# A fused gated-attention and gated-FFN kernel: a new order of all its steps, new buffers, and 309 instead of 534 dummy matmuls

## The chip, the cores and the metric

The kernel runs on one core of one Trainium2 chip. The metric is device time in microseconds (us) of one execution; lower is better. Before the change it is 286.42 us, the median of three runs (286.03 to 288.17).

Engine names in the profile: PE is TensorE (matmuls), PEld its weight loads, DVE VectorE, ACT ScalarE, POOL GpSimd, SP SyncE, which here only issues transfers. L948 means line 948 of the kernel file.

## The reference, cut to what matters

```python
def _attn_ref(q, k, v, a_re, a_im):               # 4 batches, 8 heads, 768 steps, head size 48
    mag = np.sqrt(a_re * a_re + a_im * a_im)
    scale = np.minimum(mag, 0.999) / (mag + 1e-06)
    a_re_n, a_im_n = (a_re * scale, a_im * scale)
    ...
    for t in range(S):                            # a complex decay of a 48x48 state
        ar, ai = a_re_n[:, :, t, :, None], a_im_n[:, :, t, :, None]
        new_re = ar * S_re - ai * S_im
        new_im = ar * S_im + ai * S_re
        S_re, S_im = (new_re + k[t] v[t]^T, new_im)   # shortened
        y[:, :, t] = q[t] . S_re                      # shortened

def _moe_ref(x, w_gate, w_val, w_out):            # x 3072x384, w_gate and w_val 384x1536, w_out 1536x384
    gate = 1.0 / (1.0 + np.exp(-(x @ w_gate)))
    return (gate * (x @ w_val)) @ w_out           # shortened
```

x is y with its heads put side by side. Everything is f32 at the borders.

## The kernel before

The sequence is cut into chunks of 128 steps, so there are 24 slabs (6 chunks of 4 batches). The slabs go through the FFN in groups of 1, 1, 2, 4, 4, 4, 4, 2 and 2. Each slab first goes through its attention part: loads of a_re and a_im (steps `lr`, `la`), squares and logarithms and angles on ScalarE, cumulative sums as matmuls with a triangular matrix (`cl`, `ct`), products of q and k with a magnitude (`qke`, on GpSimd, for slab 0 on VectorE) and with cosine and sine (`ks`, `qs`, on VectorE), then transposes (`tp`; from slab 13 on they are transfers) and score, state and output matmuls (`sc`, `kv`, `y`). A group then does twelve gate and twelve value blocks (`pg`, `pv`), the tanh of each gate block (ScalarE), the product (`p`, VectorE) and the output matmuls (`po`).

All of it is a list of steps, and a table gives each step one sort key. The keys are no times on the chip: the program sorts by them, and each engine gets its instructions, and SP and GpSimd their transfers, in that order.

```python
SIZES = [1, 1, 2, 4, 4, 4, 4, 2, 2]
TIMES = {"consts": [...], "wg": [28.263, 7.549, 23.318], ..., "la": [0.86, 2.2, 20.947, ...], ...}
SLOTS = {"qk": "043210341243030213403124", ...}   # which buffer each tile of a kind takes, in order
WARM = {('cl', 0): 90, ('ct', 0): 44, ..., ('pg', 7, 9): 2}   # 534 in all
...
        order = sorted(self.steps, key=lambda k: (at[k], self.rank[k]))
```

The loads, the square, and the two kinds of product that share SBUF:

```python
    def dma_in(dst, src, b, c):                          # 192 KB, issued by SP
        nc.sync.dma_start(
            heads(dst), src[b, :, c * L:(c + 1) * L].rearrange("h t d -> t h d"))
    ...
                nc.scalar.activation(out=T[SQ], in_=T[A][:, :, s],      # sq: needs lr and la
                                     func=FT.Square)
    ...
                eng(g).tensor_tensor(out=T[QK], in0=T[QK], in1=T[EE],   # qke, on GpSimd
                                     op=ALU.mult)
    ...
                    nc.vector.tensor_tensor(                            # ks and qs, on VectorE
                        out=T[SL][i].rearrange(...)[:, :, :, 0:D],
                        in0=heads(T[QK][:, i]).unsqueeze(2).broadcast_to([L, H, 2, D]),
                        in1=T[CS].rearrange("p r (h d) -> p h r d", d=D),
                        op=ALU.mult)
```

The carry of a slab to the next chunk (`hop`) is a transfer issued by GpSimd that adds into its destination ("carry transfer"). The weights come as nine blocks (`wg`, `wv`, `wo`, three each), also issued by GpSimd. The end of the program walks the order and puts dummy matmuls, zero times zero into the tile that the step is about to overwrite, ahead of some steps:

```python
        for key in order:
            ...
            for _ in range(WARM.get(key, 0)):
                nc.tensor.matmul(warm_of(tiles[st[2][0]]), zero, zero, start=True,
                                 stop=True)
            st[0](tiles)
```

They are meant to keep TensorE's clock from falling while it would wait anyway; what taking them out does is measured under b_nodum.

## Time and profile before

| | before |
|---|---|
| time, median of 3 runs | 286.42 us |
| span of the profiled run | 282.5 us |
| TensorE busy | 260.3 us in 2586 matmuls, 534 of them dummies |
| VectorE, ScalarE, GpSimd busy | 197.2, 200.3, 158.4 us |

TensorE is the bound, so what counts is the time in which it does no real work: it stands, it works at half clock, or it does dummies. The page's slices, the stretches and the largest wait are shown in the prediction below. TensorE's further waits in the kernel before (columns: who waited, for whom; us in total, times, longest us):

```profile
PE tp L824 <- DVE kst L786: 3.4, 2, 2.4
PE tp L825 <- DVE qst L786: 1.3, 2, 0.6
PE ct L741 <- ACT ee L661: 1.1, 1, 1.1
```

And the stretch from 40 to 80 us (columns: borders and length, busy us and instructions of PE, weight loads, DVE, ACT and POOL, granted clock, DMA share, GB/s):

```profile
40.00:80.00 40.00, 35.20 (x458) 29.43 (x455) 19.81 (x48) 26.29 (x53) 21.87 (x22) 0.91 0.90 160
```

PE looks well used here, but 35.20 us of busy time hold dummies and work at half clock.

### The profile page before, as it was taken

How to read it: one execution, taken by the hardware profiler on the slowest of the kernel's cores; microseconds unless marked ns; L12 is line 12 of the kernel's file. 1: busy time of each engine (PE TensorE's matmuls, PEld its weight loads, DVE VectorE, ACT ScalarE, POOL GpSimd, SP SyncE). 2: the span in 40 equal slices, each digit the busy share in tenths (PEclk: the TensorE clock that was granted, in tenths of full speed). 3: DMA queues.
4: the chain of work that ended last, by engine and by line, in shares of the span. 5: the costliest groups of instructions: out<-in, count | busy, mean ns of one | idle time of the engine just before them, and what ended most of it. 6: DMA issues, size and time to landing. Idle time of an engine off the chain costs nothing.

```text
span 282.5 us, 6759 instructions
## 1 busy us (share of the span) xinstructions
PE 260.3 (92%) x2586; PEld 179.7 (64%) x2586; DVE 197.2 (70%) x364; ACT 200.3 (71%) x340; POOL 158.4 (56%) x170
## 2 busy tenths in 40 slices
PE   8956994999998999999999999799999999998995
PEld 8735783888767766545774456454457545577784
DVE  3155553672478989898795897798788686697553
ACT  3993992478998997789953999674899559924240
POOL 0604981445968889947999717945449704803000
PEclk9999997799999999999999999999999999999999
DMA  7999999889489944596347769858997744074001
GB/s 146 200 180 194 167 200 195 170 177 207 60 116 201 208 97 57 100 212 139 83 91 121 157 134 210 143 90 129 222 218 105 127 102 102 9 150 107 30 30 56
DMA packets 175344, 38.46 MB, mean 136 GB/s; under 512 B 167992, under 2 KB 175312, under 8 KB 175312
## 3 DMA queue, kind: packets, MB, share of 16 engines
q1 hardware_dynamic: 170688, 34.46, 64.2%
q0 software_dynamic: 4624, 3.57, 8.6%
q8 instruction: 20, 0.33, 0.5%
q14 instruction: 12, 0.10, 0.1%
HBM read 31.01 MB, written 4.76 MB: 127 GB/s over the span
## 4 chain that ended last, share of the span: by engine, by line
PE 35%; ACT 22%; DMA 13%; POOL 9%; SPq 8%; issue 7%; DVE 4%; ACTq 0%; POOLq 0%; DVEq 0%
PE o L984 8%; PE g L948 8%; DMA a<-in_a_im_dram 8%; PE v L948 8%; SPq L579 6%; ACT L1012 5%; ACT sq L605 3%; PE ct L741 2%; PE cl L652 2%; ACT g L958 2%; ACT lm L632 2%; POOL lm L611 2%; DMA qkT<-qst 2%; POOL qk L714 2%; ACT cr L764 2%
## 5 line engine op out<-in xcount | busy, mean ns | idle before, releaser
L958 ACT ACTIVATE g<-g 128x512 f16<-128x512 f32 (+2 forms) x108 | 47.2, 455 | 48.8 <-PE g L948 40.8
L964 DVE SCALAR_TENSOR_TENSOR p<-g,v 128x512 f16<-128x512 f16 (+2 forms) x108 | 52.4, 506 | 32.0 <-PE v L948 15.3
L948 PE MATMUL v<-xt,wv 128*128 128x512 f16 (+2 forms) x324 | 60.9, 313 | 4.6 <-ACT g L958 4.2
L948 PE MATMUL g<-xt,wg 128*128 128x512 f16 (+2 forms) x324 | 59.9, 311 | 1.0 <-ACT g L958 0.5
L984 PE MATMUL o<-wo,p 128*128 128x384 f16 (+1 forms) x300 | 55.5, 319 | 0.0
L714 POOL TENSOR_TENSOR qk<-qk,ee 128x768 f32<-128x768 f32 x23 | 44.7, 1976 | 18.7 <-DMA qk<-in_q_dram 10.9
L611 POOL TENSOR_TENSOR lm<-sq 128x384 f32<-128x384 f32 x23 | 25.4, 1119 | 36.5 <-ACT sq L605 36.3
L948 PEld LDWEIGHTS <-wv 128*128 128x128 f16 x324 | 29.9, 100 | 22.5 <-issue 5.4
L948 PEld LDWEIGHTS <-wg 128*128 128x128 f16 x324 | 30.2, 99 | 21.6 <-issue 4.0
L1012 ACT ACT_TABLE_LOAD x31 | 39.8, 1283 | 0.5
L1018 PEld LDWEIGHTS <-zero 128*128 128x128 f16 x534 | 34.1, 102 | 5.6 <-issue 3.5
L851 DVE TENSOR_TENSOR mst<-sc,c_t 128x512 f16<-128x512 f32 x48 | 32.1, 684 | 6.6 <-PE sc L843 6.4
L984 PEld LDWEIGHTS <-p 128*128 128x128 f16 x300 | 27.0, 97 | 14.1 <-issue 0.9
L643 POOL TENSOR_TENSOR a<-a 128x768 f32<-128x768 f32 (+1 forms) x12 | 20.8, 1746 | 20.3 <-ACT a L637 15.4
L605 ACT ACTIVATE sq<-a 128x768 f32<-128x768 f32 x24 | 20.1, 841 | 14.0 <-DMA a<-in_a_im_dram 13.3
L786 DVE TENSOR_TENSOR kst<-qk,cs 128x768 f16<-128x768 f32 x24 | 23.5, 978 | 9.2 <-ACT cs L778 3.8
L786 DVE TENSOR_TENSOR qst<-qk,cs 128x768 f16<-128x768 f32 x24 | 23.4, 980 | 0.0
L741 PE MATMUL ct<-a,c_t 128*128 128x384 f32 x48 | 20.5, 512 | 1.8 <-ACT ee L661 1.1
L652 PE MATMUL cl<-lm,c_t 128*128 128x384 f32 x48 | 20.4, 514 | 0.8 <-DMA c_t<-glk_c 0.4
L831 DVE COPY qkT<-tp 128x1024 f16<-128x1024 f16 x26 | 17.5, 685 | 3.1 <-PE tp L825 3.0
L733 POOL DMA_DIRECT2D a<-cr x20 | 17.6, 1006 | 2.6 <-ACT a L721 2.2
L747 DVE TENSOR_SCALAR r<-ct 128x384 f16<-128x384 f32 x24 | 12.9, 551 | 8.1 <-PE ct L741 8.0
(64 smaller groups left out, 429.3 us busy)
## 6 DMA issues: line engine op xcount, KB each, us to landing
a<-in_a_re_dram SPq DMA_DIRECT2D x24, 192.0 KB
a<-in_a_im_dram SPq DMA_DIRECT2D x24, 192.0 KB
qk<-in_k_dram SPq DMA_DIRECT2D x24, 192.0 KB
v<-in_v_dram SPq DMA_DIRECT2D x24, 192.0 KB
qk<-in_q_dram SPq DMA_DIRECT2D x24, 192.0 KB
out_dram<-ot SPq DMA_DIRECT2D x23, 192.0 KB
wg<-in_moe_w_gate_dram POOLq DMA_DIRECT2D x3, 384.0 KB, 6.1
wv<-in_moe_w_val_dram POOLq DMA_DIRECT2D x3, 384.0 KB, 7.8
```

The lines of the kernel that those rows point to most:

```text
L605: nc.scalar.activation(out=T[SQ], in_=T[A][:, :, s], func=FT.Square)
L611: eng(g).tensor_tensor(out=T[LM][:, s], in0=T[SQ][:, 0], in1=T[SQ][:, 1], op=ALU.add)
L714: eng(g).tensor_tensor(out=T[QK], in0=T[QK], in1=T[EE], op=ALU.mult)
L741: nc.tensor.matmul(T[CT][:, :HD], wt_t, T[A][:, 1, s], start=True, stop=False, skip_group_check=True)
L786: nc.vector.tensor_tensor(out=T[SL][i].rearrange("p h (r x) -> p h r x", r=2)[:, :, :, 0:D], in0=heads(T[QK][:, i]).unsqueeze(2) .broadcas ...
L851: nc.vector.tensor_tensor(out=T[MS], in0=T[SC], in1=msk_t.unsqueeze(1).broadcast_to([L, 4, L]), op=ALU.mult)
L948: nc.tensor.matmul(T[ACC][:, :nt], w[:, j, fb * 128:fb * 128 + 128], T[XT][:, j, :nt], start=(j == 0), stop=(j == 2))
L958: nc.scalar.activation(out=T[G16][:, :nt], in_=T[PG][:, :nt], func=FT.Tanh, scale=0.5)
L964: nc.vector.scalar_tensor_tensor(out=T[PT][:, fb, :nt], in0=T[G16][:, :nt], scalar=1.0, op0=ALU.add, in1=T[PV][:, :nt], op1=ALU.mult)
L984: nc.tensor.matmul(T[PO][:, :wd], T[PT][:, fb, s * L:(s + 1) * L], wo16[:, fb, c0:c0 + wd], start=(fb == 0), stop=(fb == NFB - 1))
L1012: nc.scalar.preload_act_table_set(SETS[key[1]])
L1018: nc.tensor.matmul(warm_of(tiles[st[2][0]]), zero, zero, start=True, stop=True)
```

## The change

The intent is a new order of all steps in which VectorE's products do not stand beside runs of GpSimd instructions behind a carry transfer. Two slabs are through their attention part when the first gate block starts, and fewer dummies are needed. Only the three tables change: the keys of every kind of step, the buffers, the dummies. The diff, cut to a few of its some 330 lines:

```diff
 TIMES = {
     "wg": [
-        28.263, 7.549, 23.318],
+        34.405, 6.316, 29.967],
     "wo": [
-        37.677, 33.061, 38.497],
+        37.806, 46.233, 43.463],
     "la": [
-        0.86, 2.2, 20.947, 18.967, 22.867, 32.518, 40.682, 17.017, 57.834,
+        2.2, 0.45, 14.098, 15.058, 19.858, 17.938, 27.738, 25.755, 50.107,
     "lk": [
-        3.16, 8.421, 6.04, 23.827, 16.057, 52.074, 50.154, 48.796, 84.272,
+        7.461, 3.16, 5.08, 18.898, 56.053, 40.133, 40.543, 57.013, 62.417,
     ... (every other kind of step as well)
 SLOTS = {
-    "qk": "043210341243030213403124",
+    "qk": "043210342130420411041302",
     ...
 WARM = {
-    ('cl', 0): 90,
-    ('ct', 0): 44,
+    ('cl', 0): 11,
+    ('ct', 0): 45,
     ...
+    ('pg', 0, 11): 34,
     ... (534 to 309 in all)
```

The table grows by three lines, so a line number of the code behind it is 3 higher after: L786 becomes L789, L948 L951, L1018 L1021.

## The prediction

> **What bounds the kernel now.** I read the page's busy line and slices first, then TensorE's costs by form, its waits, the chain, and at last the order of the steps in both programs.
>
> The page says that TensorE is the bound, and the slices say where it is not at work. Columns: engine, then the busy tenths of 40 slices of 7.06 us.
> ```profile
> span 282.5 us, 6759 instructions
> PE 260.3 (92%) x2586; PEld 179.7 (64%) x2586; DVE 197.2 (70%) x364; ACT 200.3 (71%) x340; POOL 158.4 (56%) x170
> PE   8956994999998999999999999799999999998995
> PEclk9999997799999999999999999999999999999999
> DMA  7999999889489944596347769858997744074001
> ```
> Losses are in the first 57 us: there TensorE has holes, its clock falls once (slices 7 and 8), and DMA is full. From 57 us on TensorE is nearly full, and only less work on it, or fewer holes, can help.
>
> The stretches, with the borders put where I need them: 37.09 us is where the first gate block (line 948) starts. Columns after the borders: length, then busy us (instructions) of PE, weight loads, DVE, ACT, POOL, then granted clock, DMA share, GB/s.
> ```profile
> 0.00:37.09 37.09, 28.79 (x370) 24.26 (x371) 14.72 (x33) 26.82 (x40) 17.08 (x24) 1.00 1.02 180
> 37.09:60.00 22.91, 18.50 (x257) 16.64 (x256) 13.37 (x32) 11.52 (x31) 9.78 (x10) 0.85 1.09 186
> 100.00:250.00 150.00, 146.79 (x1248) 85.91 (x1246) 122.87 (x204) 117.68 (x187) 100.31 (x106) 1.00 0.67 126
> ```
> The largest single hole, from TensorE's waits and from the chain between 30 and 50 us:
> ```profile
> PE v L948 <- ACT g L958: 4.2, 1, 4.2
> ...
> 32.65 14.51 DMA a<-in_a_im_dram
> ...
> 47.23 0.84 ACT sq L605
> 48.07 0.17 ACT g L958
> 48.24 0.04 issue
> 48.29 0.80 PE v L948 x6
> ```
> A load of a_im for slab 5, issued at 32.65 us, landed 14.5 us later. ScalarE is in order: its square of that slab stood ahead of a tanh of group 0, so the tanh came at 48.07 us, and TensorE stood still for 4.2 us. The clock then fell to half from 46.25 to 53.08 us (the trace's clock records).
>
> The products on VectorE (line 786) and on GpSimd (line 714), min/median/max in ns:
> ```profile
> L786 DVE TENSOR_TENSOR kst<-qk,cs x24: 948/958/1444, 18.7 to 248.6; 128x768 f16<-128x768 f32 x24
> L714 POOL TENSOR_TENSOR qk<-qk,ee x23: 1805/1819/2618, 22.4 to 244.1; 128x768 f32<-128x768 f32 x23
> ```
> The longest kst product started at 111.86 us within a qk product of GpSimd, was followed on GpSimd by a carry transfer (line 733) that ended at 113.23, and itself ended at 113.31.
>
> **What the Trainium skill says.** Three places.
> "SBUF — State Buffer", section "Who interferes with whom": a VectorE instruction with two SBUF inputs contends with a GpSimd instruction that reads SBUF, and the later one waits. The trace agrees: 4 of the 48 kst and qst products are long (1026, 1196, 1404 and 1444 ns against 950 to 960), each beside GpSimd work.
> "TensorE: Matmul & The Clock Gate", Part 1: the clock halves after an idle window of about 3.4 us and comes back after a busy one; 128-column matmuls then start 107 against 56 ns apart. The trace agrees: dummies start 107 ns apart until 5.3 us, then 56; the half-rate record lasts 6.83 us after the 4.2 us hole.
> "DMA: Bandwidth & Descriptors", "Issuing engines are not separate DMA queues": what SP and GpSimd issue runs on the same DMA engines and interleaves. Here that is the cause of the 14.5 us: five weight blocks from GpSimd were issued from 30.3 to 40.0 us.
>
> **The change part by part.** No operation of the computation changes: all 2052 real matmul passes stay, and so do the 364 VectorE instructions. What changes is the order of every engine's queue, the buffers, the dummies (534 to 309) and ScalarE's table loads (31 to 28). I use the keys of the step table for order alone.
>
> *Cost of TensorE's work.* From the groups by form, at back-to-back pace: a gate or value block of three matmuls is 0.647 us at 512 columns, 0.328 at 256, 0.167 at 128; four output matmuls 0.650; cl and ct 0.70 each; the smaller ones 0.16 to 0.45. Summed over all steps that is 218.9 us. Dividing it at the first gate block by the order of steps gives 9.0 + 209.9 us before the change, 10.3 + 208.6 us after it, since slab 1 is now through its attention part when the gates start.
>
> *Dummies.* They fill 33.0 us, 0.062 us each. Placed before/after the first gate: 289/245 now, 118/191 in the new order. Those before the first gate fill time in which TensorE waits anyway and cost nothing; the 54 fewer after it save 54 x 0.062 = 3.3 us, as they stand for waits that the new order is meant not to have.
>
> *The kernel before as a sum.* 37.1 to the first gate + 209.9 real + 245 x 0.062 = 15.2 dummies + 6.5 slow matmuls (busy 231.5 after the first gate, less the two; 2.4 of them are the 4.8 us worked at half clock) + 4.2 the hole + 6.3 other holes + 3.3 from the last matmul to the end = 282.5.
>
> *First gate.* Before, it waits for its activations; its weights had landed at 15.3 us. After, the first gate block is number 11, so it needs the third block of w_gate. In the order of issue 26 loads of 192 KB and 4 weight blocks come up to and with it. The page's queue rows (64.2% of the span for 34.46 MB, 8.6% for about nine weight blocks) make 1.03 us per load and 2.7 per block: 2.0 + 26 x 1.03 + 4 x 2.7 = 39.6. The same sum for the first block of w_gate before (23 loads, 4 blocks) gives 36.5, and it landed at 36.0. So 39.1, and the gate starts at about 39.3: **2.2 us later**, an estimate.
>
> *The hole.* The last load of slab 5 is SP's 23rd transfer instead of its 33rd and comes ahead of all but two weight blocks; it will not stop a tanh. That takes 4.2 us of hole and 2.4 us of half clock. But the later weight blocks are now tight: w_gate's first block should land at 41.5 to 42.5 with its user due near 41.5, w_val's second near 44.5 with its user due then, v of slab 3 later than its GpSimd cast. I put 2.0 us of new waits there.
>
> *VectorE and GpSimd apart, fewer table loads.* The four long products lose 1.3 us in all, mostly off TensorE's path; three table loads are 3 x 1.28 us of ScalarE. Such delays reach TensorE as part of the 6.3 us of small holes (1.1 us before a ct at 180, 1.0 before sc at 259). I take 2 us off, a choice and not a calculation.
>
> *Sum.* 39.3 + 208.6 + 191 x 0.062 = 11.8 + (6.5 - 2.4) = 4.1 + 2.0 + 4.3 + 3.3 = 273.4 us of span, 9.1 less. The timed median is 286.4 - 9.1 = **277.3 us**, 3.2% faster.
>
> **Rivals.**
> *The hole comes back elsewhere.* The loads are issued later and nearer to their use: a_re to its square is 7.7 instead of 11.8 apart in the key table on average. With DMA full until 60 us, one late block of 4 us would bring the half clock again: 2 + 2.4 us more than my sum, so about 282. For it: DMA share above 1.0. Against it: fewer weight blocks at once around 32 us.
> *TensorE goes cold before the first gate.* 171 dummies fewer there, and none in the first 7 us. Half clock from 17 to 30 us would slow little real work (some 4 us of it), but could push the first gate by 1 to 2 us: 279. Against it: the weights that the gate waits for are late anyway, and 34 dummies stand just before it.
> *DMA bounds the start, so the order gains nothing there.* Then only the dummies after 60 us and small holes are won, 3 to 4 us: 283, within 2%.
> *All waits vanish.* Without the 2.0 and with smaller holes: 273.
>
> **Range and chances.** The two gains that I can point at, 6.6 us of hole and clock and 3.3 us of dummies, are set against 2.2 + 2.0. The rivals lie between 273 and 283, so 273 to 282. The 2% line is 280.7, some 3.4 us above my number; two rivals cross it. Faster 0.84, within 2% 0.14, slower 0.02.
>
> **What would show it.** First gate block near 39.3 us; no TensorE wait over 3 us and no half clock between 35 and 60 us; TensorE busy about 16 us less (225 dummies and the slow matmuls); long kst and qst products gone; 150 us from 100 to 250 as full as before. It is wrong if a DMA stops ScalarE or GpSimd for over 3 us before 65 us, or if TensorE's small holes after 60 us grow.

## The result, and the profile after

Ratios here are the mean time of one kernel's fast runs over that of the other's in the same rounds, so not quite the ratio of the medians that are quoted. A run counts as slow when it is over 1.5% above the fastest of its kernel.

After the change the median is **276.48 us** (four runs, 275.01 to 279.03); before, in the same rounds, 287.3 us (286.03 to 293.3). The ratio of fast runs is 0.9647, with a 95% interval of 0.9546 to 0.9748: 3.5% faster. The span of the profiled run went from 282.5 to 274.6 us. The page of the kernel after:

```profile
span 274.6 us, 6298 instructions
PE 246.6 (90%) x2361; PEld 166.2 (61%) x2361; DVE 205.3 (75%) x364; ACT 196.3 (71%) x337; POOL 168.7 (61%) x170
PE   0766697998979999899999999999999999999995
PEclk9995999999999999999999999999999999999999
DMA  7989999999759583599574987679986367640011
```

TensorE is busy 13.7 us less, all of it dummies or slow matmuls. The half clock has moved from slices 7 and 8 to slice 4, before the first gate. (No clock record covers the time up to 11.58 us, up to 5.29 before; the dummies there start 107 ns apart, as at half clock.) VectorE and GpSimd are busy 8 and 10 us *longer*, with the same 364 and 170 instructions as before: single instructions got longer. The stretches up to the first gate block (40.63 us) and over the same 40 us as above:

```profile
0.00:40.63 40.63, 24.84 (x261) 18.96 (x262) 18.73 (x38) 30.68 (x47) 23.01 (x27) 0.92 0.99 178
40.63:60.00 19.37, 17.28 (x230) 14.47 (x228) 11.39 (x29) 16.06 (x33) 8.34 (x9) 1.00 1.21 198
```
```profile
40.00:80.00 40.00, 36.39 (x446) 29.26 (x443) 27.82 (x57) 33.42 (x69) 27.46 (x27) 1.00 1.00 163
```

TensorE is busy only 1.2 us more from 40 to 80 us than before, yet real work for 26.5 instead of 21.1 us ends there. ScalarE and VectorE do 7 and 8 us more in the stretch, and the DMA share rises from 0.90 to 1.00, which fits slabs that are prepared earlier. The same sum, from the start of the program:

```text
real matmul work ended by (us):    40     60     80    100    150    200    250   all
before                           10.2   20.2   31.3   47.0   94.2  141.6  190.3  218.9 at 279.23
after                            10.2   22.6   36.7   52.1   98.3  146.5  196.6  218.9 at 271.38
```

(Worked out by giving each real matmul its back-to-back cost from the groups by form, and adding up those that ended.) Nothing is won by 40 us, though the first gate starts 3.5 us later. By 80 us the lead is 5.4 us, and it stays between 4.1 and 6.3 us until 250 us and is 7.9 us at the end. The lead arises in the 40 us in which slabs 2 and 3 are prepared: they are the first group of two slabs, and its first gate block (256 columns) starts at 70.05 instead of 78.97 us. That of the first group of four slabs starts at 105.25 instead of 111.88 us.

TensorE's waits after:

```profile
PE cl L655 <- ACT lm L635: 10.1, 4, 8.4
PE tp L828 <- DVE qst L789: 3.4, 3, 2.0
PE tp L827 <- ACT cr L767: 1.5, 1, 1.5
PE v L951 <- DVE p L967: 1.2, 2, 1.0
```

The first is at the very start, where the kernel before had dummies. The 4.2 us for a tanh is gone, and behind the first gate none lasts longer than 2.0 us. But that one is new, and it is of the kind that the change was to remove. The products after (columns: min/median/max in ns, first and last start, shapes), and VectorE's and GpSimd's timelines where the longest of these waits is made:

```profile
L789 DVE TENSOR_TENSOR kst<-qk,cs x24: 940/974/2072, 19.2 to 233.1; 128x768 f16<-128x768 f32 x24
L789 DVE TENSOR_TENSOR qst<-qk,cs x24: 944/950/2557, 20.0 to 240.6; 128x768 f16<-128x768 f32 x24
L717 POOL TENSOR_TENSOR qk<-qk,ee x23: 1802/2049/2916, 16.1 to 216.2; 128x768 f32<-128x768 f32 x23
```
```profile
77.72 1.55 DVE L789 TENSOR_TENSOR kst<-qk,cs 128x768 f16<-128x768 f32 x1 [0.28 <-ACT cs L781]
79.18 2.56 DVE L789 TENSOR_TENSOR qst<-qk,cs 128x768 f16<-128x768 f32 x1
```
```profile
77.63 0.82 POOL L621 TENSOR_SCALAR lm<-lm 128x768 f32<-128x768 f32 x1
78.53 2.40 POOL L717 TENSOR_TENSOR qk<-qk,ee 128x768 f32<-128x768 f32 x1
```

The longest product was 1444 ns before; it is 2557 ns now. Taken over 951 ns each, the 48 products were 1.4 us too long before (four of them) and are 9.5 us too long after (nineteen of over 1000 ns, from 22 to 233 us). The growth of 8.1 us is all that VectorE is busy longer. The timelines show one case: the qst product starts at 79.18 inside GpSimd's qk product, which runs to 80.93, and ends only at 81.74, about one product's length after that. TensorE's transpose of this slab starts at 81.80 us, after 2.0 us of standing.

### The profile page after: what moved, and what is told of

Its sections match the earlier page's. It is cut to its first block, busy times and chain, and to the rows that moved or that the text cites.

```text
span 274.6 us, 6298 instructions
## 1 busy us (share of the span) xinstructions
PE 246.6 (90%) x2361; PEld 166.2 (61%) x2361; DVE 205.3 (75%) x364; ACT 196.3 (71%) x337; POOL 168.7 (61%) x170
## 4 chain that ended last, share of the span: by engine, by line
PE 53%; DVE 9%; ACT 4%; issue 4%; POOL 2%; DMA 1%; SPq 1%; DVEq 0%; ACTq 0%
PE o L987 13%; PE g L951 12%; PE v L951 12%; PE ct L744 4%; PE cl L655 3%; PE sc L846 2%; DVE p L967 2%; DVE qst L789 2%; POOL qk L717 1%; DVE mst L854 1%; PE y L912 1%; DMA qk<-in_q_dram 1%; PE y L914 1%; DVE kst L789 1%; PE xp L932 1%
## 5 line engine op out<-in xcount | busy, mean ns | idle before, releaser
L967 DVE SCALAR_TENSOR_TENSOR p<-g,v 128x512 f16<-128x512 f16 (+2 forms) x108 | 52.1, 503 | 16.6 <-ACT g L961 8.3
L951 PE MATMUL v<-xt,wv 128*128 128x512 f16 (+2 forms) x324 | 60.4, 308 | 1.3 <-DVE p L967 1.2
L951 PE MATMUL g<-xt,wg 128*128 128x512 f16 (+2 forms) x324 | 59.2, 308 | 0.8 <-DVE ot L543 0.4
L717 POOL TENSOR_TENSOR qk<-qk,ee 128x768 f32<-128x768 f32 x23 | 47.0, 2119 | 7.8 <-ACT ee L664 6.2
L951 PEld LDWEIGHTS <-wg 128*128 128x128 f16 x324 | 28.9, 97 | 20.2 <-issue 3.2
L951 PEld LDWEIGHTS <-wv 128*128 128x128 f16 x324 | 28.8, 97 | 20.0 <-issue 4.0
L614 POOL TENSOR_TENSOR lm<-sq 128x384 f32<-128x384 f32 x23 | 26.3, 1146 | 22.4 <-ACT sq L608 22.1
L1015 ACT ACT_TABLE_LOAD x28 | 35.9, 1283 | 0.5
L987 PEld LDWEIGHTS <-p 128*128 128x128 f16 x300 | 26.9, 98 | 13.2 <-issue 0.7
L655 PE MATMUL cl<-lm,c_t 128*128 128x384 f32 x48 | 21.2, 532 | 10.4 <-ACT lm L635 10.1
L789 DVE TENSOR_TENSOR kst<-qk,cs 128x768 f16<-128x768 f32 x24 | 27.7, 1153 | 3.7 <-POOL qk L717 3.1
L646 POOL TENSOR_TENSOR a<-a 128x768 f32<-128x768 f32 (+1 forms) x12 | 21.8, 1832 | 12.1 <-ACT a L640 10.1
L789 DVE TENSOR_TENSOR qst<-qk,cs 128x768 f16<-128x768 f32 x24 | 27.4, 1143 | 0.0
L1021 PEld LDWEIGHTS <-zero 128*128 128x128 f16 x309 | 21.1, 103 | 4.9 <-issue 3.4
L778 ACT ACTIVATE cs<-ct 128x384 f32<-128x384 f32 x24 | 11.8, 490 | 11.5 <-PE ct L757 11.3
```

What stands on the lines that cost most here:

```text
L614: eng(g).tensor_tensor(out=T[LM][:, s], in0=T[SQ][:, 0], in1=T[SQ][:, 1], op=ALU.add)
L646: eng(g).tensor_tensor(out=T[A][:, 1, i:j], in0=T[A][:, 1, i:j], in1=T[A][:, 0, i:j], op=ALU.mult)
L655: nc.tensor.matmul(T[CL][:, :HD], wl_t, T[LM][:, s], start=True, stop=True)
L717: eng(g).tensor_tensor(out=T[QK], in0=T[QK], in1=T[EE], op=ALU.mult)
L789: nc.vector.tensor_tensor(out=T[SL][i].rearrange("p h (r x) -> p h r x", r=2)[:, :, :, 0:D], in0=heads(T[QK][:, i]).unsqueeze(2) .broadcas ...
L951: nc.tensor.matmul(T[ACC][:, :nt], w[:, j, fb * 128:fb * 128 + 128], T[XT][:, j, :nt], start=(j == 0), stop=(j == 2))
```

## The experiments

The theory after the result: *the order of transfers in the DMA-full first 60 us makes the gain, because it lets the first two-slab group be prepared earlier.* Its rivals: the 225 dummies less make it; the later, warmer first gate makes it; DMA bounds the start whatever the order, so a wait taken away comes back at the next load. A second question is what the long products cost. Twelve runs were made in three batches, two of them of the unchanged kernel after as controls; all gave right results. "Ratio" is to the kernel before in the same rounds.

| label | kernel | ratio, 95% interval | median us |
|---|---|---|---|
| b_la5 | before, one load moved ahead | none: one fast run | 287.1 |
| b_nodum | before, no dummies behind first gate | 0.9976 (0.994 to 1.0013) | 285.37 |
| b_order | before, three transfers moved | 0.985 (0.9796 to 0.9904) | 280.59 |
| a_late7 | after, one load moved back | 0.9873 (0.9811 to 0.9936) | 281.63 |
| a_nodum | after, no dummies behind first gate | 0.9775 (0.9713 to 0.9837) | 278.67 |
| a_few34 | after, 8 dummies at first gate for 34 | 0.9822 (0.9743 to 0.9901) | 278.4 |
| a_warm | after, 40 dummies more at the start | 0.9893 (0.9838 to 0.9948) | 279.9 |
| a_again | after, unchanged, second batch | 0.9719 (0.9592 to 0.9846) | 279.38 |
| a_again2 | after, unchanged, third batch | 0.9703 (0.9649 to 0.9758) | 276.43 |
| a_pool | after, three GpSimd steps moved | 0.9828 (0.9777 to 0.9879) | 278.29 |
| a_pool2 | after, two GpSimd steps moved | 0.9667 (0.9608 to 0.9726) | 275.16 |
| a_best | a_pool2 with 24 dummies more at the start | 0.9743 (0.9691 to 0.9795) | 277.48 |

The second batch (a_again, a_few34, a_warm, a_pool; on another chip than the first and third) was noisy, and only two of the six runs of its control counted as fast; so comparisons between versions of the kernel after rest on the third batch where they can. The first batch (b_la5, b_nodum, a_late7, a_nodum) had no control of the kernel after.

### b_la5: the load that made the 4.2 us hole, moved ahead

```diff
-        0.86, 2.2, 20.947, 18.967, 22.867, 32.518, 40.682, 17.017, 57.834,
+        0.86, 2.2, 20.947, 18.967, 22.867, 27.500, 40.682, 17.017, 57.834,
```

> The kernel before with one transfer moved: a_im of slab 5 is issued right behind a_re of slab 5, ahead of the weight blocks. Theory (the 4.2 us hole and the 2.4 us that the half clock took were lost for good): TensorE has no wait over 3 us between 40 and 60 us, no half clock there, and the kernel is 4 to 6.5 us faster (ratio 0.977 to 0.986). Rival (DMA bounds this stretch whatever the order): the wait comes back at the square of slab 6, whose loads are the next behind the weight blocks, and the gain is 0 to 2 us (ratio 0.993 to 1.0).

Measured: 281.2 to 289.6 us in six runs, median 287.1; five count as slow beside the one at 281.2, so there is no ratio, and no gain can be read. The mean of all six is 286.45 us against 286.12 for all runs of the kernel before beside them. The profile fell in a slow run; it is read for the kind of wait, not for its length. Its chain from 33 to 50 us (start us, us, what):

```profile
33.13 8.97 DMA qk<-in_q_dram
...
42.26 1.82 POOL qk L714
44.08 0.02 issue
44.10 0.96 DVE kst L786
45.06 2.35 DVE qst L786
47.40 0.05 issue
47.45 0.29 PE tp L825
```

The tanh is no longer stopped. Now the q load of another slab, issued behind the a_im load at 33.13 instead of 31.51 us, takes 9.0 us and holds up GpSimd, VectorE and then TensorE, with holes of 1.4 and 2.1 us and the half clock (45.97 to 52.79 us) as before. So the rival fits this edit, though it named the square of slab 6 and the wait came at a q load: moving one transfer alone in a full stretch moved the wait to another load.

### b_order: three transfers of the kernel before moved

The k load of slab 4 (not used before 60 us) and the second block of w_out go back, the a_im load of slab 5 goes ahead of them, and the string of "qk" buffers is reordered with it: by the order of the k loads, slab 4 keeps buffer 2 and every other slab its own.

```diff
 "wo":
-        37.677, 33.061, 38.497],
+        37.677, 38.000, 38.497],
 "la":
-        0.86, 2.2, 20.947, 18.967, 22.867, 32.518, 40.682, 17.017, 57.834,
+        0.86, 2.2, 20.947, 18.967, 22.867, 29.000, 40.682, 17.017, 57.834,
 "lk":
-        3.16, 8.421, 6.04, 23.827, 16.057, 52.074, 50.154, 48.796, 84.272,
+        3.16, 8.421, 6.04, 23.827, 50.600, 52.074, 50.154, 48.796, 84.272,
 SLOTS:
-    "qk": "043210341243030213403124",
+    "qk": "043103241243030213403124",
```

> The kernel before with three transfers moved: k of slab 4, not used before 69 us in its table, from 16.1 to 50.6; the second block of w_out behind its first; a_im of slab 5 behind q of slab 2, ahead of the weight blocks. Theory (what cost the time was the order of the transfers: early loads that nobody needs yet put those needed behind them): neither the wait of 4.2 us nor the 3.5 us of b_la5 comes, no half clock between 43 and 55 us, and it is 3 to 6 us faster than before (ratio 0.979 to 0.99). Rival (DMA bounds the stretch whatever the order, so the gain of the change came from elsewhere): ratio 0.995 or more, with a new wait on a load.

Measured: 280.59 us (279.12 to 282.1, all fast), ratio 0.985; in means 280.64 against 284.92 us, **4.3 us less**. TensorE's waits:

```profile
PE tp L824 <- DVE kst L786: 2.4, 1, 2.4
PE ct L741 <- DMA a<-cr: 1.9, 1, 1.9
PE tp L825 <- DVE qst L786: 1.1, 2, 0.6
```

The 4.2 us for the tanh is gone and so is the half clock from 46 to 53 us. The 1.9 us for a carry transfer at 72.65 us are new, and half clocks of 3.4 us came at 19.5 and, behind that wait, at 74.1 us. Nothing was removed and no dummy changed, so the order of transfers is worth some 4 us by itself. By 60 us as much real work has ended as in the kernel after (22.6 us, by the same sum); then b_order falls behind (about 33.0 against 36.7 us by 80). By 100 us it is 50.4 us, against 47.0 before and 52.1 after. Its first two-slab gate starts at 76.50 us.

### a_late7: one load of the kernel after moved back

```diff
 "lr":
-        0.86, 0.04, 13.138, 16.018, 16.978, 21.778, 28.983, 31.83, 44.144,
+        0.86, 0.04, 13.138, 16.018, 16.978, 21.778, 28.983, 39.750, 44.144,
```

> The kernel after with one transfer put back behind weight blocks: a_re of slab 7 is issued behind v of slab 3. It should land near 49 us, its square is due near 43.4. Theory (a late load in ScalarE's order stops the tanh behind it and then TensorE, and the loss stays): a wait of TensorE of 4 to 6 us near 44 us, a half clock of 6.8 us after it, and 4 to 7 us slower than after (ratio 0.98 to 0.99). Rival (TensorE makes such a hole up by fewer dummies and waits later): at most 2 us slower (ratio 0.972 or less).

Measured: ratio 0.9873, median 281.63 us (279.6 to 283.08), 1.5 to 2.3% above the three ratios of the kernel after, some 4 to 6 us, though these were taken in other batches (with a_again's the intervals overlap). One line of the chain, and one of TensorE's waits:

```profile
40.02 10.79 DMA a<-in_a_re_dram
```
```profile
PE g L1021 <- ACT g L961: 5.9, 1, 5.9
```

This is the wait of the kernel before, made again: a load takes 10.8 us, the square of that slab stands ahead of a tanh in ScalarE's queue, TensorE stands still for 5.9 us, and the clock halves (48.17 to 55.0 us). The first gate of the first two-slab group came at 77.29 instead of 70.05 us. So in both programs one late load of the stretch costs 4 to 6 us.

### b_nodum and a_nodum: no dummies behind the first gate

245 dummies less in the kernel before, 157 less in the kernel after:

```diff
-    ('pg', 0, 9): 3,
-    ... every entry of WARM whose step comes behind the first gate block
```

> The kernel before without the 245 dummy matmuls behind the first gate block. Prediction's step (dummies stand for waits that TensorE has anyway, so that taking them out alone gains nothing and only fewer waits do): the time within 1% of before, TensorE busy 15 us less and its holes 15 us more, unless the clock falls between 60 and 80 us, which would cost 2 to 4 us. Rival (the dummies stand in TensorE's way): 2 to 3.3 us faster.

> The kernel after without the 157 dummies behind the first gate block (those before it and just ahead of it stay). Same question as for the kernel before: within 1% of after (ratio 0.955 to 0.975) if they stand for waits, with one more stretch of half clock possible between 50 and 90 us for 2 to 4 us; 1 to 2.5 us faster than after (ratio 0.957 or less) if they stand in TensorE's way.

Measured: b_nodum 0.9976, the same within 0.6%; a_nodum 0.9775, no faster than the kernel after in any batch. TensorE had 245 matmuls, some 15 us at full clock, less to do, and the time did not move. In b_nodum's profile (a slow run) TensorE's holes behind the first gate are 24.1 us against 10.6 before: taking the dummies out gives the waits back. It was busy only 6.2 us less, not the 15 that I expected, for the clock was at half for 23.9 us against 6.8 before. The fast runs show the same: their granted clock was 0.958 to 0.976 instead of 0.975 to 1.0. The rival "fewer dummies make it" is ruled out for those behind the first gate. No run takes out the 171 before it; the real work ended by 40 us is 10.2 us in both kernels.

### a_few34: an earlier first gate

```diff
-    ('pg', 0, 11): 34,
+    ('pg', 0, 11): 8,
```

> The kernel after with 8 instead of 34 dummies ahead of the first gate block. If these dummies, begun late, hold the first gate block up beyond the landing of its weights: gate block at 39.3 to 39.6 us, about 1 us faster than the control. If they only fill a wait: no change, or slower by a later half clock.

Measured: ratio 0.9822, 278.4 us, against 0.9719 and 279.38 us for the unchanged kernel beside it: no gain that these runs resolve. TensorE's timeline:

```profile
38.84 0.50 PE L951 MATMUL g<-xt,wg 128*128 128x128 f16 x6
42.24 0.27 PE L827 MATMUL tp<-c_t,kst 128*128 128x128 f16 x1 [2.90 <-ACT cr L767]
```

The gate starts at 38.84 instead of 40.63 us, does two blocks, and then TensorE waits 2.90 us for ScalarE. The products that the next transposes read had ended at 41.71 us; the wait ends with ScalarE's `cr` step, which stands behind `cs` steps and a square, and so the transposes come only 0.35 us earlier than in the kernel after (42.24 against 42.59). So an earlier first gate, the milestone that my prediction hung its sum on, is used up at the next wait. The missing gain has a second cause that this run does not part from it: with fewer dummies the clock was at half from 41.90 to 45.31 us, which the kernel after does not have there.

### a_warm and a_best: the half clock before the first gate

Dummy transposes ahead of two steps of slabs 0 and 1, 20 each in a_warm, 12 each in a_best (which has a_pool2's edit too):

```diff
+                if key[0] == "tp":
+                    nc.tensor.transpose(warm_of(tiles[st[2][0]]), zero, idn_t)
+                    continue
```

> The kernel after with 40 more dummies (transposes of zeros) ahead of two of the first transposes, at about 19.6 and 22.2 us. Theory (the clock falls there because TensorE has only about a third of a window busy, and the 1.4 us that it costs delay the first gate block): no half clock between 15 and 35 us, first gate block at 39.3 to 39.8 us instead of 40.6, 0.7 to 1.5 us faster than the control. Rival (the third block of w_gate, landed at 39.3, and what follows it bound the start): under 0.5 us.

> a_pool2 with 24 dummy transposes ahead of two early transposes, so that the clock does not fall at 22 us. If both losses count: 0.5 to 1.5 us faster than a_pool2. If ScalarE's work on slabs 2 and 3 bounds the start: no difference to a_pool2.

Measured: a_warm 0.9893, above its control (0.9719); a_best 0.9743, which is 2.4 us *above* a_pool2 in the means of the same batch (277.60 against 275.21). The half clock at 22 us vanished and came at 32.0 to 35.4 us (a_warm) and 29.75 to 36.58 us (a_best), and the first gate came later: 41.30 us in a_warm, and 42.07 in a_best against 40.16 in a_pool2. So the cold clock before the first gate is not worth curing in this way. Why the cure costs 2.4 us is not settled: the dummies may hold up transposes that others wait for. TensorE was busy for 1.57 of the 3.41 us before the clock fell, nearly half and not the third that I wrote in the expectation.

### a_pool and a_pool2: GpSimd steps out of the way of long products

A magnitude product (`qke` of slab 7) and two additions of squares are moved in GpSimd's order; a_pool2 leaves the first addition where it was and moves the product a little further.

```diff
 "qke":
-        14.708, 15.668, 35.225, 31.742, 68.189, 59.356, 61.697, 75.626,
+        14.708, 15.668, 35.225, 31.742, 68.189, 59.356, 61.697, 77.390,   (a_pool2: 78.180)
 "add":
-        65.938, 70.299, 78.172, 79.127, 105.136, 83.988, 101.268, 115.549,
+        67.400, 70.299, 78.172, 79.127, 105.136, 83.988, 102.230, 115.549,   (a_pool2: 65.938 stays)
```

> The kernel after with three GpSimd steps put behind the VectorE products that they held up: the qk product of slab 7 behind the state update of slab 4, the lm sum of slab 15 behind the cast of v of slab 9, the lm sum of slab 9 behind the carry of slab 7. Theory (GpSimd work that reads SBUF blocks kst and qst, and in this kernel that reaches TensorE: 2.0 us at 80 us, 1.0 us at 110 us): those two waits of TensorE gone, the longest qst no longer 2.6 us, and 1.5 to 3 us faster than the control. Rival (the time is made up elsewhere; TensorE's holes there would be filled by other waits): less than 0.7 us.

> The kernel after with two GpSimd moves that do not put new work behind a carry transfer: the qk product of slab 7 behind the lm sum of slab 11, the lm sum of slab 15 behind the cast of v of slab 9 (the lm sum of slab 9, whose move made a qst 4.3 us long in a_pool, stays in its place). Theory: no TensorE wait of 1 us or more between 60 and 115 us, no half clock near 84 us, 2 to 3.5 us faster than the control. Rival (other waits come in their place): under 1 us.

> The kernel after, unchanged, as the control of this batch: 0.960 to 0.970 of before. In its profile the half clock before the first gate (21.8 to 28.65 us in the first trace) comes back or not; if it is there in every trace it belongs to the order, if not to the phase of the clock's window.

> The kernel after, unchanged, as the control of this batch: 0.96 to 0.975 of before, with the wait of 2.0 us for a qst near 80 us.

Measured: a_pool 0.9828 against 0.9719 for its control in fast runs, but 278.29 against 279.38 us in the medians of all runs: no gain that this batch resolves. The move of the later addition did what it should, and the hole at 110 us went. The move of the first one put it behind a carry transfer, and a product fell into that run; VectorE's timeline, then GpSimd's:

```profile
71.99 4.26 DVE L789 TENSOR_TENSOR qst<-qk,cs 128x768 f16<-128x768 f32 x1
```
```profile
71.84 0.80 POOL L736 DMA_DIRECT2D a<-cr  x1
72.44 1.23 POOL L614 TENSOR_TENSOR lm<-sq 128x384 f32<-128x384 f32 x1
73.40 2.02 POOL L717 TENSOR_TENSOR qk<-qk,ee 128x768 f32<-128x768 f32 x1
```

The product starts inside the carry transfer, waits through two GpSimd instructions that start after it, and ends 0.8 us after the last of them: 4.26 us for 0.95 us of work, and 2.03 us of hole on TensorE. This is what the change was meant to avoid, shown by accident. a_pool2, without that move, ran at 275.16 us (274.17 to 277.1), in means 275.21 against 276.47 us for the unchanged kernel in the same batch. Its longest wait for a product is halved, and the 1.0 us for `p` at 110 us is gone:

```profile
PE tp L828 <- DVE qst L789: 2.5, 3, 1.0
```

1.26 us in the means, less than the 2 to 3.5 us that I expected, with ranges that overlap: suggested, not shown. It is the fastest version measured. The 2.0 us hole for the long product near 80 us stands in both controls, as expected, and can cost more than itself: behind it the clock halved for 3.4 us in the profiles of a_again (from 84.04 us), a_again2 (81.66), a_few34 and a_warm, though not in that of the kernel after; of the three kernels with the moved product (a_pool, a_pool2, a_best) none has it. The half clock before the first gate came in both controls too (from 22.60 us in a_again, 23.64 in a_again2), so it belongs to the order; its length differs.

## Why the prediction was right or wrong

The time (277.3 predicted, 276.48 measured) and the direction were right. My sum, against the profile after:

| term (us) | predicted | after |
|---|---|---|
| start to first gate, with the 34 dummies before it | 41.4 | 40.6 |
| real matmuls behind it | 208.6 | 208.6 (not measured apart) |
| dummies and slow matmuls behind it | 13.8 | 13.2 |
| holes behind it (new DMA waits + others) | 2.0 + 4.3 | 9.0 |
| tail | 3.3 | 3.3 |
| span | 273.4 | 274.6 |

The measured column: 40.63 from the stretches; TensorE's busy time behind it is 221.8 us, less 208.6 of real work; holes are the rest up to the last matmul at 271.38. The prediction booked the 34 dummies, 34 x 0.062 = 2.1 us, behind the gate; they stand before it, and are moved here (39.3 + 2.1, and 11.8 - 2.1 + 4.1).

- **First gate and weights.** Sized well: the third block of w_gate landed at 39.30 us, estimated 39.1. But it was the wrong milestone. a_few34 brought the gate forward by 1.8 us and won nothing measurable, and between before and after it came 3.5 us later in the faster kernel with as much real work done by 40 us.
- **The hole and its half clock.** Right, and the largest single cause that the runs show: the 4.2 us hole and the half clock behind the first gate are gone, b_order takes them out of the kernel before with three transfers for 4.3 us, and a_late7 puts them back into the kernel after for 4 to 6 us. I had sized them at 6.6 us. One reading of mine was wrong: I took the trace to agree that the clock falls after about 3.4 us of idling, but it fell at 46.25 us, when TensorE had stood for 2.2 us.
- **The dummies.** The 3.3 us came out in the sum, but were no cause. (TensorE was busy 13.7 us less, not 16.) The prediction itself says that dummies stand for waits; the runs without them show it.
- **New DMA waits of 2.0 us: wrong in kind.** TensorE waits for no weight block behind the first gate, and no half clock falls between 35 and 60 us, although DMA is as full (share 1.21 from 40.63 to 60 us).
- **"Long kst and qst products gone": the step that failed.** I took the change's intent for its effect and booked the products' 1.3 us among 2 us of small holes saved. The excess grew from 1.4 to 9.5 us. Why is open: in b_order, whose first two-slab gate comes 2.5 us earlier than before, it is only 1.5 us, and the long products after the change are spread over the whole kernel. TensorE paid 2.0 us at 80 and 1.0 us at 110 us (the `p` behind a qst product of 2.23 us). Holes other than the tanh's went from 6.4 to 9.0 us instead of down to 4.3. Most of that growth, 1.9 us, lies between the first gate and 60 us, 1.5 of it in the wait for ScalarE's `cr` at 42.59 us, for which my sum has no term. Behind 60 us they grew from 6.2 to 6.9 us, which the prediction had itself named as a sign of being wrong. So the number stayed near by luck: of the 4.7 us too many, 2.0 were set aside for DMA waits that did not come, and the first gate and the slow matmuls took 1.4 less than I gave them.
- **Rivals.** "The hole comes back elsewhere" and "DMA bounds the start" did not happen, yet b_la5 shows that both are real for an order that moves one load only. "TensorE goes cold before the first gate" happened (half clock from 21.82 to 28.65 us), and it cost no more than the first-gate term allowed.

Left open: b_order accounts for some 4 us of the 8 to 10 us, and no run splits the rest. By 60 us b_order and the kernel after are level, so the rest is won later: the lead over b_order is about 3.7 us of work by 80 us, 1.7 by 100, and its last matmul ends 4.2 us later (275.59 us). That this too comes from earlier preparation is argued from the traces only. Whether a_pool2 beats the new order, and why a_best is slower, is not settled either.

## What to carry to other kernels

Measure progress as real work ended by a given time, not as the start of a milestone or as busy time, since dummies and half clock count as busy. In a stretch where DMA is full, moving one load ahead may only hand the wait to another, as in b_la5; ask which transfer is not needed yet and put that one back. An order meant to keep two engines apart has to be checked in the trace, product by product: here the products' excess grew from 1.4 to 9.5 us under an order meant to remove it.

## What the Trainium skill lacked or had wrong

- "TensorE: Matmul & The Clock Gate", Part 1: it gives an idle window of about 3.4 us as what halves the clock (a later section tells of frequent short idle times that make the clock change, but gives no number for them). No idle window was needed here: in the 3.41 us before the clock fell in the kernel after, TensorE was busy for 1.57 us, and its longest standstill was 0.65 us. No run gives a border. With windows of 3.41 us counted on from the clock records, the clock stayed full after one with 1.46 us busy (kernel after, the hole at 80 us), and fell after others with 1.47 us (a_again2) and 1.88 us (a_nodum). Two windows of the kernel after, the first followed by half and the second by full clock:

```profile
18.41:21.82 3.41, 1.57 (x17) 0.87 (x16) 3.12 (x4) 2.61 (x7) 0.17 (x2) 1.00 0.77 153
...
79.85:83.26 3.41, 1.46 (x18) 1.31 (x19) 3.41 (x5) 1.67 (x4) 3.41 (x3) 1.00 1.11 222
```

- "SBUF — State Buffer", "Who interferes with whom": it says that the order of issue decides who blocks and, of VectorE's two-port modes, that the first keeps the shared pair for the whole instruction. The 4.26 us product of a_pool began before two GpSimd instructions and still ended after both; the page does not tell of a wait through several instructions.
- "ScalarE: Activation LUTs", "What ACT_TABLE_LOAD costs": it puts a drain of about 1380 ns beside the load's 1283 ns. The trace agrees with the 1283 ns, but shows no drain between a load and its neighbours: of the 28 loads of the kernel after, all begin within 0.03 us of the end of the activation before, and the next one begins within 0.02 us in 24 cases. So the estimate of 1.28 us per load that the prediction used stands.
